# Column layout of the projection banks in a Hedgehog-attention plus MLP kernel, and one transpose for the later row statistics

## The chip, the cores and the metric

The kernel runs on one core of one Trainium2 chip. The metric is the device time of one launch in microseconds (us). The kernel before the change was run three times: 738.21, 738.29 and 739.31 us, median 738.29 us.

## What is computed

One layer over 2048 tokens of width 640 computes `x + attention(layernorm(x)) + mlp(layernorm(layernorm(x)))`; the second normalisation is the MLP's own.

```python
# attention: 32 heads of 20 features; the feature map is learned per head
qkv = x @ wqkv                                   # 640 -> 3 * 640
pq, pk = q @ w_phi[h], k @ w_phi[h]              # 20 x 20 per head
phi = concat(softmax(p), softmax(-p))            # 40 features per head, for q and k
kv, z = phi_k^T v, sum(phi_k)                    # over all tokens: no causal mask
o = (phi_q kv) / (phi_q z + 1e-6);  return o @ wo
# MLP: 640 -> 1728, tanh GELU, 1728 -> 640, with biases
```

## The kernel before

**Folding.** The 20 x 20 feature maps are folded into the projection weights, so that one matmul gives the map's input to the softmax. A softmax does not change when one feature is subtracted from all, so feature 0 is subtracted from the other 19 in the weights and is a constant zero: each head of q and of k is a projection of 19 columns (`DF`), and v one of 20. That gives 608 + 608 + 640 = 1856 projection columns.

**Precision.** Each fp32 operand is split into a high and a low fp32r part, the high by ScalarE (L54), the low by VectorE or GpSimd (L57). `mm3` (L62 to L65) is one product as three matmuls: high times high, high times low, low times high. Every product of 128 rows is thus three matmuls, and 640 rows are 15.

**Stages, in order of time.** (1) To about 36 us: load x, normalise, transpose the first 1024 tokens, first MLP chunks. (2) To about 225 us: the MLP over tokens 0 to 1023 (two blocks of 512, 14 hidden chunks in pairs). TensorE runs one `mm3` per kc step, and after each step calls `next(self.beside)` (L246, L288): one step of a generator that lays the preparation of the attention in between. One step of 512 columns is three matmuls. (3) From 225 to 447 us: the projections, 16 tiles of 128 tokens (L698 to L735). (4) From 447 us: the MLP over tokens 1024 to 2047, with attention, quotients and the output projection.

**The preparation generator** (`prep`, L478) runs in stage 2. For k and then q it takes six groups of six heads (the last of two), folds them (`prep_fold`, L443: matmuls of 114 columns into a bank of `Banks(3, 4)`, a split of each bank) and yields three times per half bank. The folded k goes to the resident weights `wkv_`, as does q's first group; the rest of q goes by way of a tile `t` (two buffers) to DRAM and comes back into `wq_` before stage 3 (L569 to L573). In between, statistics of the tokens 1024 to 2047 (`more_stats`). Then five chunks of v's weights are loaded into `raw` (two buffers) and split. Last, for b = 2 and 3, `rows` (L179): mean and reciprocal deviation of 512 tokens, which lie one per partition, are transposed on TensorE, copied out, stored to DRAM (L190) and loaded back broadcast to all partitions as `mr` (L192); and for each of five chunks of 128 features of x^T: load into `raw` (L508), subtract the mean on GpSimd (L518), multiply on VectorE (L521), high part on ScalarE (L525) and low part on VectorE (L528) into the two halves of a `t` tile, both stored to `y_dram` (L530). They come back as `y[b]` during stage 3.

In stages 1 and 2 the order of the instructions of TensorE, VectorE, ScalarE and GpSimd is that of the program text (`manual_schedule`, L302 and L352): an instruction that waits holds up all behind it on its engine. The DMAs all go through SyncE's queue (SP), whose order a scheduler sets; from stage 3 to the second pair of hidden chunks of stage 4 (L1007) it also sets the order on VectorE, ScalarE and GpSimd.

**A tile of stage 3** has four projections `proj(t, i)` (L585), each into one of three PSUM banks (0, 1, 2) that take turns, and, two tiles late, the product of the k features with v (`kv_tile`, L656): ten matmuls of 240 columns into banks 3 to 7 and one of 160 into the ring of three. With `CB` (L26) the four banks hold:

- i = 0: 24 heads of k (456 columns)
- i = 1: 8 heads of k (152) and 15 heads of v (300)
- i = 2: 17 heads of v (340) and 6 heads of q (114)
- i = 3: 26 heads of q (494), from `wq_`

ScalarE copies q and k from PSUM to `pks` (`evacuate`, L610; rows of 20 with feature 0 left at zero), ScalarE and VectorE split v (L652, L654). `k_tile` follows i = 1, `q_tile` the last bank with q. Both call `features` (L612): maximum and minimum per head on VectorE (L617, L618), differences on GpSimd (L628), exponential on ScalarE (L629), sums on VectorE (L631). The last tiles run as (13,0) (13,1) (13,2) (14,0) (14,1) (13,3) (15,0) (15,1) (14,3) (15,3) (14,2) (15,2), so that the last two `q_tile` come after their i = 2. The first pass of stage 4 is issued on ScalarE after the exponential of q of tile 15 (L776), and GpSimd's clearing of `kvs` and two weight splits after that tile's differences (L748, L796, L1001).

## Time and profile before

| | us |
|---|---|
| median of three runs | 738.29 |
| span of the profiled execution, first to last instruction | 736.8 |
| TensorE busy in the span | 723.8 |
| VectorE / ScalarE / GpSimd busy | 479.9 / 320.5 / 370.6 |
| stage 3 (225 to 447): VectorE / ScalarE / GpSimd busy, of 222.0 | 177.8 / 107.1 / 172.5 |

The profile gives no time outside the span; the median of the runs is 1.5 us above it. Times in the profile count from the first instruction. Matmuls are pipelined: a matmul's row is longer than its turn, so what one costs is read as the distance from one start to the next, and TensorE's busy time hides short waits. In a timeline row the bracket is the idle time before the instruction and what ended it. PE is TensorE, DVE VectorE, ACT ScalarE, POOL GpSimd, SP the queue of DMA issues.

### The profile page before, as it was taken

The page shows a single profiled execution, that of the slowest core. Times are in us where ns is not written, and L with a number is a line of the kernel's source. Part 1 is how long each engine was busy: PE and PEld are TensorE (multiplying, and loading weights), DVE is VectorE, ACT ScalarE, POOL GpSimd, SP SyncE. Part 2 cuts the span into 40 slices and gives each one's busy share as a digit, 9 for nine tenths or more (in the row PEclk, how much of TensorE's full clock was granted, in tenths as well). Part 3 has the DMA queues.
Part 4 walks back from the last instruction along what each step waited for, and adds up shares of the span by engine and source line. Part 5 has one row for each costly group of instructions (what it writes and reads, how often), then busy time and mean ns, then how long its engine had stood idle before and what let it go on. Part 6 is the DMA issues. An engine that isn't in the chain of part 4 may idle for free.

```text
span 736.8 us, 9681 instructions
## 1 busy us (share of the span) xinstructions
PE 723.8 (98%) x3441; PEld 610.2 (83%) x3441; DVE 479.9 (65%) x790; ACT 320.5 (44%) x526; POOL 370.6 (50%) x322
## 2 busy tenths in 40 slices
PE   9999999998999999999999999999999999999998
PEld 7788888777788998998998888888878888877886
DVE  7847645665653788788888788645575656767331
ACT  6624444332322464464345357256565556440110
POOL 2211222343321797797778889445586777304000
PEclk9999999999999999999999999999999999999999
DMA  9704477464543223633600706853433353153222
GB/s 317 221 19 141 143 177 178 141 193 142 159 161 144 75 86 144 161 101 150 143 0 1 179 1 200 196 149 107 126 116 114 113 157 90 48 215 127 83 84 73
DMA packets 64520, 95.36 MB, mean 129 GB/s; under 512 B 13312, under 2 KB 35216, under 8 KB 62848
## 3 DMA queue, kind: packets, MB, share of 16 engines
q1 hardware_dynamic: 64184, 94.74, 42.5%
q8 instruction: 27, 0.44, 0.3%
q14 instruction: 21, 0.17, 0.1%
q10 hardware_dynamic: 288, 0.01, 0.0%
HBM read 64.47 MB, written 30.26 MB: 129 GB/s over the span
## 4 chain that ended last, share of the span: by engine, by line
PE 73%; DVE 10%; DMA 5%; POOL 5%; ACT 3%; issue 3%; SPq 0%; POOLq 0%; DVEq 0%; ACTq 0%
PE bank L63 22%; PE bank L65 21%; PE bank L64 21%; PE bank L659 2%; PE bank L456 2%; POOL m L628 2%; PE bank L882 1%; DMA m<-r 1%; PE bank L881 1%; DVE acc L295 1%; DVE y L946 1%; DVE rx L925 1%; DVE m L57 1%; DMA raw<-in_wv 1%; DMA xb<-in_x 1%
## 5 line engine op out<-in xcount | busy, mean ns | idle before, releaser
L57 POOL TENSOR_TENSOR w<-r,w 128x640 fp32r<-128x640 f32 x52 | 83.2, 1618 | 107.6 <-ACT w L54 77.4
L63 PE MATMUL bank<-y,w 128*128 128x512 f32 (+1 forms) x334 | 131.1, 392 | 0.9 <-ACT m L250 0.6
L65 PE MATMUL bank<-y,w 128*128 128x512 f32 (+1 forms) x334 | 129.8, 389 | 0.3 <-POOL w L57 0.3
L64 PE MATMUL bank<-y,w 128*128 128x512 f32 (+1 forms) x334 | 129.6, 388 | 0.0
L63 PE MATMUL bank<-m,w 128*128 128x512 f32 x260 | 104.3, 401 | 4.6 <-DVE acc L295 3.8
L65 PE MATMUL bank<-m,w 128*128 128x512 f32 x260 | 101.8, 392 | 0.0
L64 PE MATMUL bank<-m,w 128*128 128x512 f32 x260 | 101.7, 391 | 0.0
L295 DVE TENSOR_TENSOR acc<-bank,acc 128x512 f32<-128x512 f32 x120 | 80.7, 682 | 16.7 <-PE bank L65 11.1
L57 DVE TENSOR_TENSOR m<-m,m 128x512 fp32r<-128x512 f32 (+1 forms) x54 | 45.0, 834 | 67.1 <-ACT m L54 67.1
L63 PE MATMUL bank<-wkh,y 128*128 128x456 f32 (+2 forms) x240 | 88.6, 369 | 0.0
L64 PE MATMUL bank<-wkl,y 128*128 128x456 f32 (+2 forms) x240 | 88.5, 369 | 0.0
L65 PE MATMUL bank<-wkh,y 128*128 128x456 f32 (+2 forms) x240 | 88.4, 368 | 0.0
L63 PEld LDWEIGHTS bank<-y,w 128*128 128x128 f32 x334 | 62.8, 188 | 14.1 <-DVE ob L1050 0.8
L65 PEld LDWEIGHTS bank<-y,w 128*128 128x128 f32 x334 | 62.7, 188 | 13.8 <-POOL w L57 0.7
L64 PEld LDWEIGHTS bank<-y,w 128*128 128x128 f32 x334 | 62.8, 188 | 12.7
L610 ACT ACTIVATE m<-bank 128x456 f32<-128x456 f32 (+3 forms) x64 | 27.0, 422 | 94.6 <-PE bank L65 78.2
L628 POOL TENSOR_TENSOR m<-m,mx 128x640 f32<-128x640 f32 (+2 forms) x48 | 44.5, 941 | 46.4 <-DVE mx L617 46.4
L63 PEld LDWEIGHTS bank<-m,w 128*128 128x128 f32 x260 | 48.9, 188 | 18.3 <-DVE acc L295 6.9
L875 POOL TENSOR_TENSOR e<-e,m 120x512 fp32r<-120x512 f32 (+1 forms) x28 | 38.1, 1362 | 43.2 <-ACT m L874 41.2
L65 PEld LDWEIGHTS bank<-m,w 128*128 128x128 f32 x260 | 48.8, 188 | 10.6
L631 DVE TENSOR_REDUCE sm<-m 128x64 f32<-128x1280 f32 x32 | 47.2, 1476 | 15.6 <-ACT m L629 15.5
L64 PEld LDWEIGHTS bank<-m,w 128*128 128x128 f32 x260 | 48.9, 188 | 9.6
(156 smaller groups left out, 1397.8 us busy)
## 6 DMA issues: line engine op xcount, KB each, us to landing
r<-in_w SPq DMA_DIRECT2D x52, 320.0 KB
e<-e SPq DMA_DIRECT2D x40, 240.0 KB
e<-acc SPq DMA_DIRECT2D x52, 160.0 KB
acc<-in_xT SPq DMA_DIRECT2D x4, 1280.0 KB
xb<-in_x SPq DMA_DIRECT2D x8, 320.0 KB
t<-in_x SPq DMA_DIRECT2D x8, 320.0 KB
raw<-in_xT SPq DMA_DIRECT2D x10, 256.0 KB
yh<-t SPq DMA_DIRECT2D x10, 256.0 KB
```

Source lines behind the costliest of these rows:

```text
L57: eng.tensor_tensor(lo, src, f(hi), op=ALU.subtract)
L63: nc.tensor.matmul(ps, lh, rh, start=first, stop=False, **kw)
L64: nc.tensor.matmul(ps, lh, rl, start=False, stop=False, **kw)
L65: nc.tensor.matmul(ps, ll, rh, start=False, stop=last, **kw)
L295: nc.vector.tensor_tensor(acc[b][:, m, :], pw, acc[b][:, m, :], op=ALU.add)
L456: nc.tensor.matmul(ps[:, i * kd:(i + 1) * kd], raw[:kk, (k + i) * P:(k + i + 1) * P], wpt[:kk, g, :kd // DF, 1:], start=True, stop=True)
L610: return nc.scalar.activation(p3[:, h:h + src.shape[1], 1:], src, AF.Copy).ins
L628: subs[n, t] = nc.gpsimd.tensor_tensor(ep[:, s], a, b, op=ALU.subtract)
L631: nc.vector.tensor_reduce(sm, e.rearrange("p s (h f) -> p (s h) f", f=DH), axis=AX, op=ALU.add)
L659: nc.tensor.matmul(kvp[g // 2][:VM, (g % 2) * 240:(g % 2) * 240 + 240].rearrange("p (s f) -> p s f", s=4), v[:, g * VS:g * VS + VM], ft[:, ...
L875: nc.gpsimd.tensor_tensor(pl, e, f(ph), op=ALU.subtract)
L881: nc.tensor.matmul(pn, kvs[:w, g, :], ph, start=True, stop=False)
```

## The change

The four banks of a tile get new contents. Of the 19 folded features of each head, 16 of k fill bank 0 (512 columns), and 16 of q bank 3 (512). The last 3 features of k (96 columns) and of q (96) stand in bank 1 with 15 heads of v (492 in all), and bank 2 has only v (340). `evacuate` copies a range of features of all 32 heads; bank 1 now has two such copies. `q_tile` follows i = 3 for every tile.

The preparation makes this layout: each folded half bank takes two splits, one of 16 and one of 3 features per head. All of q's first 16 features now go by way of DRAM, the rest stands in `wkv_`.

The rows of both later blocks are transposed once, as 16 rows, directly after the folding and ahead of v's weights, stored once and loaded back by two broadcasts, into tiles of their own (the second in one of the two buffers of `t`). The ten chunks of x^T run in one loop; the high part goes to one of the two halves of a `t` tile that is held throughout, and the low part is written over the chunk itself in `raw`, from where it is stored.

```diff
-CB = [24 * DF, QK + 15 * DH, QK + D + G5, 2 * QK + D]
+F1, F2 = 16 * H, 3 * H
+CB = [F1, F1 + 2 * F2 + 15 * DH, F1 + 2 * F2 + D]
...
-    def rows(b, xp, ptile):
-
-        sc = xp.tile([P, 2, 4], F32, name="sc", bufs=1)
-        nc.vector.tensor_copy(sc[:, 0, :], mv[:, 4 * b:4 * b + 4, 0])
-        nc.vector.tensor_copy(sc[:, 1, :], ry[:, 4 * b:4 * b + 4])
-        for _ in range(2):
+    def rows(xp, ptile):
+
+        sc = xp.tile([P, 2, 2, 4], F32, name="sc", bufs=1)
+        nc.vector.tensor_copy(sc[:, :, 0, :], mv[:, 8:16, 0].rearrange("p (b t) -> p b t", b=2))
+        nc.vector.tensor_copy(sc[:, :, 1, :], ry[:, 8:16].rearrange("p (b t) -> p b t", b=2))
+        for _ in range(4):
             yield
         ps = ptile()
-        nc.tensor.transpose(ps[:8, :P], sc.rearrange("p a t -> p (a t)"), idt)
...
+        nc.tensor.transpose(ps[:16, :P], sc.rearrange("p b a t -> p (b a t)"), idt)
...
+        nc.sync.dma_start(r_dram, sr)
+
+    def row_pair(b, mr):
+
+        nc.sync.dma_start(mr, r_dram[8 * b - 16:8 * b - 8].rearrange("r t -> (r t)").unsqueeze(0).to_broadcast([P, 8 * P]))
+        return mr.rearrange("p (a t) -> p a t", a=2)
...
-            split(dst[0][:, k:k + ni], dst[1][:, k:k + ni], ps[:, :ni * kd].rearrange("p (i f) -> p i f", i=ni))
+            src = ps[:, :ni * kd].rearrange("p (i h f) -> p i h f", i=ni, f=DF)
+            split(*[w[:, k:k + ni].rearrange("p c (h f) -> p c h f", f=16) for w in dst], src[:, :, :, 0:16])
+            split(*[w[:, k:k + ni, c3:c3 + 3 * nh].rearrange("p c (h f) -> p c h f", f=3) for w in wkv_], src[:, :, :, 16:])
             for _ in range(3):
                 yield
-        if n == "q" and g:
+        if n == "q":
             for p in range(2):
-                nc.sync.dma_start(wq_dram[p][:, :, (g - 1) * G5:(g - 1) * G5 + kd], f(t[:, p]))
+                nc.sync.dma_start(wq_dram[p][:, :, 96 * g:96 * g + 16 * nh], f(dst[p]))
...
+        finish(more)
+        yield from rows(fp, mlp.px)
+        hi_lo = fp.tile([P, 2, KC, G5], F32R, name="t").rearrange("p a c f -> p a (c f)")
+        mrs = [row_pair(2, mtile(5).rearrange("p a t -> p (a t)")),
+               row_pair(3, fp.tile([P, 2, KC, G5], F32, name="t").rearrange("p a c f -> p (a c f)")[:, :8 * P])]
...
-        for b in range(2, 4):
-            mr = yield from rows(b, fp, mlp.px)
-            ahead = load(b, 0)
-            for _ in range(7):
-                yield
...
-                hl = fp.tile([P, 2, KC, G5], F32R, name="t").rearrange("p a c f -> p a (c f)")[:, :, :512]
-                nc.scalar.activation(hl[:, 0], xc, AF.Copy)
-                for _ in range(2):
-                    yield
-                nc.vector.tensor_tensor(hl[:, 1], xc, f(hl[:, 0]), op=ALU.subtract)
-                for p in range(2):
-                    nc.sync.dma_start(y_dram[b - 2][p][:, c, :], f(hl[:, p]))
-                yield
+        todo = [(b, c) for b in range(2, 4) for c in range(KC)]
+        ahead = load(*todo[0])
+        for _ in range(3):
+            yield
+        for i, (b, c) in enumerate(todo):
+            mr = mrs[b - 2]
+            xc, ahead = ahead, load(*todo[i + 1]) if i < 9 else None
+            nc.gpsimd.tensor_tensor(xc, xc, mr[:, 0], op=ALU.subtract)
+            for _ in range(3):
+                yield
+            nc.vector.tensor_tensor(xc, xc, mr[:, 1], op=ALU.mult)
+            for _ in range(2):
+                yield
+            hi = hi_lo[:, i % 2, :512]
+            nc.scalar.activation(hi, xc, AF.Copy)
+            for _ in range(2):
+                yield
+            nc.vector.tensor_tensor(xc.bitcast(F32R), xc, f(hi), op=ALU.subtract)
+            for p, src in enumerate((f(hi), xc)):
+                nc.sync.dma_start(y_dram[b - 2][p][:, c, :], src)
+            yield
...
         if i == 0:
-            evac = evacuate(ps, 0, 0)
+            evac = evacuate(ps, 0, slice(1, 17))
         elif i == 1:
-            evac = evacuate(ps[:, :8 * DF], 0, 24)
-            v_parts(t, (ps[:, 8 * DF:], 0, 5, G3))
+            evac = evacuate(ps[:, :F2], 0, slice(17, 20))
+            evacuate(ps[:, F2:2 * F2], pq, slice(17, 20))
+            v_parts(t, (ps[:, 2 * F2:], 0, 5, G3))
             fts[t] = k_tile(t)
         elif i == 2:
-            evac = evacuate(ps[:, 17 * DH:], pq, 0)
             v_parts(t, (ps[:, :15 * DH], 5, 5, G3), (ps[:, 15 * DH:17 * DH], 10, 1, 2 * DH))
         else:
-            evac = evacuate(ps, pq, 6)
-        if i == (3 if t < 14 else 2):
+            evac = evacuate(ps, pq, slice(1, 17))
             q_tile(t)
```

46 lines of the change are left out of this document (17 added, 29 removed).

## The prediction, made before the result was known

> **What bounds the kernel now.** I read the page first (how busy is which engine), then what TensorE waits for, window by window, then start distances of its matmuls, then the chains around the places where it waits.
>
> ```profile
> span 736.8 us, 9681 instructions
> PE 723.8 (98%) x3441; PEld 610.2 (83%) x3441; DVE 479.9 (65%) x790; ACT 320.5 (44%) x526; POOL 370.6 (50%) x322
> ```
>
> TensorE is the bound: 98% of the span. So an edit gains only by making its matmuls take shorter turns or by removing a wait of TensorE; work taken from or put on another engine costs nothing as long as TensorE does not wait for it. The busy time by stage:
>
> ```profile
> 36.00:120.00 84.00, 83.44 (x420) 69.00 (x419) 45.66 (x103) 32.01 (x60) 15.46 (x10) 1.00 0.49 129
> 120.00:218.00 98.00, 93.77 (x410) 75.73 (x409) 59.26 (x86) 35.88 (x56) 35.87 (x26) 1.00 0.52 163
> 225.00:447.00 222.00, 221.66 (x1129) 199.39 (x1128) 177.79 (x256) 107.14 (x168) 172.51 (x171) 1.00 0.32 94
> ```
>
> The columns are length, then TensorE, weight loads, VectorE, ScalarE, GpSimd, then the granted clock, which is 1.00 throughout. The projections (225 to 447) have no hole worth naming. The window 120 to 218, in which the statistics' rows and the chunks of x^T are prepared, has 4.2 us of idle TensorE. Its waits there are few (total, times, longest), and the starts beside the three that matter:
>
> ```profile
> PE bank L63 <- DVE acc L295: 2.4, 3, 1.6
> PE bank L187 <- DVE sc L183: 1.5, 2, 1.2
> ```
>
> ```profile
> 129.81 0.39 PE L65 MATMUL bank<-m,w 128*128 128x512 f32 x1
> 131.45 0.27 PE L187 MATMUL bank<-idt,sc 128*8 128x128 f32 x1 [1.24 <-DVE sc L183]
> ...
> 165.96 0.39 PE L65 MATMUL bank<-y,w 128*128 128x512 f32 x1
> 166.65 0.27 PE L187 MATMUL bank<-idt,sc 128*8 128x128 f32 x1 [0.30 <-DVE sc L183]
> ...
> 176.77 0.39 PE L65 MATMUL bank<-m,w 128*128 128x512 f32 x1
> 178.79 0.50 PE L63 MATMUL bank<-m,w 128*128 128x512 f32 x1 [1.63 <-DVE acc L295]
> ```
>
> A matmul of 512 columns takes a turn of 0.23 us (worked out below), so the start distances 1.64, 0.69 and 2.02 hold 1.41, 0.46 and 1.79 us of waiting, **3.66 us** together. The first two are the two transposes of rows: TensorE, in program order, stands before L187 until VectorE has made `sc`. The third is the second block's broadcast:
>
> ```profile
> 175.02 2.57 POOL L518 TENSOR_TENSOR raw<-raw,m 128x512 f32<-128x512 f32 x2 [7.08 <-DMA m<-r]
> ```
>
> GpSimd waited 7.08 us for `mr`; VectorE's multiply L521 stood behind that, and the accumulation L295, which frees TensorE's bank, behind the multiply.
>
> **The change, part by part.**
>
> (a) *Bank widths.* The matmul count (60 a tile) and the columns (1856) stay. What may change is the overhead of each matmul. Starts of the first matmul of five successive groups of 15 (452, 454, 494, 456 columns, then the next), and two starts 15 matmuls of 512 apart:
>
> ```profile
> 255.00 0.40 PE L63 MATMUL bank<-wkh,y 128*128 128x452 f32 x1
> ...
> 258.12 0.36 PE L63 MATMUL bank<-wkh,y 128*128 128x454 f32 x1
> ...
> 261.20 0.38 PE L63 MATMUL bank<-w,y 128*128 128x494 f32 x1
> ...
> 264.57 0.37 PE L63 MATMUL bank<-wkh,y 128*128 128x456 f32 x1
> ...
> 267.68 1.29 PE L659 MATMUL bank<-w,v 128*127 128x240 f32 x10
> ```
>
> ```profile
> 195.92 0.39 PE L63 MATMUL bank<-y,w 128*128 128x512 f32 x1
> ...
> 199.32 0.39 PE L271 MATMUL bank<-y,w 128*128 128x512 f32 x1
> ```
>
> Turns: 3.12/15 = 208 ns at 452, 3.08/15 = 205 at 454, 3.37/15 = 225 at 494, 3.11/15 = 207 at 456, and 3.40/15 = 227 at 512. From 454 to 494 a column costs 0.49 ns; from 494 to 512 only 0.11. So 512 columns, a full bank and whole rows of 2 KB, are about 6 ns cheaper than the line through the odd widths (494 at 225 plus 18 columns at 0.44 = 233). The narrow side, from the chain of waits in order of time:
>
> ```profile
> 132.47 2.16 DMA r<-sr
> ...
> 146.04 3.94 DMA raw<-in_xT
> ...
> 169.94 4.92 DMA m<-r
> ...
> 253.96 1.12 PE bank L659 x10
> 267.84 1.12 PE bank L659 x10
> ...
> 416.20 3.15 DMA e<-acc
> ```
>
> Ten matmuls of 240 columns take 1.12 us, 112 ns each with their weight loads, so 340 columns meet no floor: from 112 at 240 and 205 at 454 (0.435 ns a column) they take 156 ns. 492 takes 224. A tile's 60 matmuls now take 3.12 + 3.08 + 3.37 + 3.11 = 12.68 us; after, 15 x (227 + 224 + 156 + 227) = 12.51. Bounds: with 512 at 231 to 233 ns nothing is gained; with 340 at 150 and 492 at 220 some 0.25 us. I take 0.12 a tile, times 16: **-1.9 us** (0 to -4.0).
>
> [...]
>
> Does the rest of a tile keep up? A period is 267.84 - 253.96 = 13.88 us and VectorE is busy 178 of 222 us, GpSimd 173: covered, by 20%. The copies on ScalarE move the same 1216 columns in four instructions. Of the bank ring, bank 1 loses: it must be free after i = 2 and i = 3, 3.08 + 3.37 = 6.45 us now, 15 x (156 + 227) = 5.75 then. Cost taken: nothing; if VectorE's low part of v comes over 2 us late, some tenths a tile.
>
> (b) *Rows in one go, directly after the folding.* Both waits for `sc` and the wait behind the second broadcast go: **-3.66 us**. The broadcasts (4.92 us) now start ahead of v's five chunks, some 15 steps before they are used; a step is three matmuls, 0.68 us, so 10 us. What is late next? Two things. v's loads share the DMA engines with 1 MB of broadcasts and stand on SP's queue beside a load that waits for the rows' store (2.16 us); behind a late chunk stands L57 on VectorE, and behind it L295.
>
> And the low part now lies in `raw`: the next load into that buffer waits until the store has landed, not only until L528 is done. The store of 256 KB to DRAM is not shown as a duration; the nearest rows are stores of 4 KB (2.16 us) and of 160 KB (3.15 us). I take 2.3, near the small one, since the store of 160 KB (`store_phi`) writes runs of 512 bytes and this one runs of 2 KB; bounds 2.0 and 4. The relay from one use of a buffer to its next is then: L528, store, load, L518, L521, L525, L528.
>
> ```profile
> L518 POOL TENSOR_TENSOR raw<-raw,m x10: 1280/1291/1752, 138.4 to 196.8; 128x512 f32<-128x512 f32 x10
> L521 DVE TENSOR_TENSOR raw<-raw,m x10: 677/683/2039, 139.8 to 200.1; 128x512 f32<-128x512 f32 x10
> L525 ACT ACTIVATE t<-raw x10: 616/634/635, 141.8 to 200.9; 128x512 fp32r<-128x512 f32 x10
> L528 DVE TENSOR_TENSOR t<-raw,t x10: 675/682/1233, 145.0 to 204.0; 128x512 fp32r<-128x512 f32 x10
> ```
>
> 2.3 + 3.94 + 1.29 + 0.68 + 0.63 + 0.68 = 9.5 us, and about 1 us for other instructions ahead on VectorE and for semaphores: 10.5. The program gives two turns of 8 steps, 16 x 0.68 = 10.9 us. So it just holds on average, but its store and load (6.24 us) do not fit in the 9 steps less L528 between (5.4), so GpSimd starts about 0.8 us late and, after the 0.75 us of slack ahead of L521, VectorE a little. I take **+0.8 us** for both (bounds 0 and +12). The three shorter waits in this window, 1.1 us by their brackets, I leave as they are.
>
> [...]
>
> (c) *End of the projections.* `q_tile` of tile 15 starts after i = 3, not i = 2.
>
> ```profile
> 439.63 0.58 ACT L610 ACTIVATE m<-bank 128x494 f32<-128x494 f32 x1 [0.29 <-PE bank L65]
> ...
> 446.08 0.25 ACT L610 ACTIVATE m<-bank 128x114 f32<-128x114 f32 x1
> ...
> 453.55 1.28 ACT L250 ACT_TABLE_LOAD   x1
> ```
>
> ```profile
> 455.58 0.51 PE L63 MATMUL bank<-y,w 128*128 128x512 f32 x1 [0.55 <-ACT m L250]
> ```
>
> Its last input comes at 439.6 instead of 446.1, 6.5 us earlier; the first GELU waits for its exponential and TensorE 0.55 us for the GELU. GpSimd is nearly full there, so the exponential gains less than 6.5 us, but 0.55 suffices. Against it, the last banks are 1.5 us shorter together, so that v of tile 14 must be split within one bank of 340 before `kv_tile`. I take **-0.5 us** (-0.7 to +1).
>
> (d) *Twice the splits in the folding.*
>
> ```profile
> L54 ACT ACTIVATE wkh<-bank 128x456 fp32r<-128x456 f32 x6 | 3.3, 553 | 18.5 <-PE bank L456 18.5
> L54 ACT ACTIVATE wkh<-bank 128x114 fp32r<-128x114 f32 x6 | 1.6, 260 | 5.5 <-PE bank L456 5.5
> ```
>
> ```profile
> L57 DVE TENSOR_TENSOR wkl<-bank,wkh 128x456 fp32r<-128x456 f32 x6 | 3.8, 630 | 5.8 <-ACT wkh L54 3.7 <-issue 2.1
> L57 DVE TENSOR_TENSOR wkl<-bank,wkh 128x114 fp32r<-128x114 f32 x6 | 1.6, 270 | 0.7 <-ACT wkh L54 0.7
> ```
>
> From the two widths an instruction's fixed part is 553 - 456 x 0.857 = 162 ns on ScalarE and 150 on VectorE. 24 more on each are 3.9 and 3.6 us, spread over 84 us in which they are busy 32 and 46: hidden behind TensorE's matmuls, except where VectorE is already late: **+0.2 us** (0 to +1). If the cover were gone, 3.6. Two more stores for q's first group ride on SP and cost nothing.
>
> Sum: -1.9 - 3.66 + 0.8 - 0.5 + 0.2 = -5.1 us on a span of 736.8; against the median of 738.29, taking the 1.5 us around the span as constant, **733.2 us**.
>
> **The rivals.** *Rival 1, no gain from the widths*: all of (a) is nothing, as where 512-wide turns cost 232 here (the stationary operand and the address are others than in the MLP). For it: same columns, same count. Against: 227 is the steady value of the 512-wide groups. 735.1 us. *Rival 2, the rows' gain is given back*: lateness of v's loads or of the relay makes TensorE wait as long as the 3.66 us removed; with (a) 736.0, together with rival 1 about 738. For it: GpSimd's 7.08 us above was a wait for a DMA, and the change adds waits for DMAs. *Rival 3, slower*: the relay takes x us over its 10.9. The ten chunks are four relays after the first two, and about 2 us of lateness are absorbed by the three banks of the second products, so it costs 4x - 2. It outweighs the 5.9 us of the rest from x = 2.0, a relay of 12.9 us, as with a store of 3.15 us, a load of 4.9 and 1 us of queue on GpSimd behind weight splits. At x = 3.5: 12 - 5.9 = +6.1, 744.4 us. Against it: load 3.94 and store near 2.16 where nothing else moves. *Rival 4*: the change doesn't do what it says, TensorE's waits for `sc` only move: within rival 2.
>
> **How the numbers follow.** Forecast (733.2, spread 730 to 734.5) 0.45; rival 1 0.17; rival 2 0.13 alone (736.0, to 737) and 0.11 with rival 1 (738); rival 3 0.14. 0.2%, about what a measurement of this kernel can tell from no change, is 1.5 us: faster means under 736.8, slower over 739.8. Faster: 0.45 + 0.17 + 0.09 = 0.71; same: 0.04 + 0.11 = 0.15; slower 0.14. The range 729.5 to 739.5 leaves out rival 3 and some 0.04 below.
>
> **What would show it.** (a) A tile's period 13.88 becomes about 13.76, with 512-wide starts 227 ns and 340-wide 156 ns apart. (b) No wait of over 0.3 us at the one transpose; no idle GpSimd before L518 for `m<-r`; idle before L518 for `raw<-in_xT` of about 1 us each. (c) No wait for L250 near 455. Wrong would make it: 512-wide turns of 232 (rival 1), waits `PE bank L63 <- DVE acc L295` in 120 to 190 that sum to over 4 us (rivals 2, 3), or a wait of TensorE for a bank in the projections.

## The result and the profile after

The changed kernel takes **739.32 us** (median of 20 runs, 738.65 to 742.56), the kernel before 738.19 us beside it (20 runs, 737.26 to 739.61): ratio 1.0016, 95% interval 1.0008 to 1.0023. So it is no faster, if anything 1.1 us slower, and not 5.1 us faster as forecast. The lines below have moved by one to ten: L54 of before is L55, L57 is L58, L63 to L65 are L64 to L66, L129 is L130, L293 is L295, L295 is L297, L456 is L459, L518 is L528, L639 is L647, L654 is L662, L659 is L667.

The head of the page of after:

```profile
span 737.6 us, 9732 instructions
...
PE 721.1 (98%) x3440; PEld 603.5 (82%) x3440; DVE 480.2 (65%) x811; ACT 324.3 (44%) x550; POOL 368.6 (50%) x322
```

TensorE's share looks unchanged, and that is all that the head can say: it is an average over stages that went in opposite directions. Busy time by stage of after, with the columns as before:

```profile
36.00:120.00 84.00, 80.39 (x398) 66.75 (x397) 46.84 (x120) 33.52 (x80) 15.44 (x10) 0.98 0.43 124
120.00:218.00 98.00, 95.60 (x419) 77.88 (x418) 60.93 (x86) 36.79 (x59) 34.92 (x25) 1.00 0.50 168
225.00:447.00 222.00, 220.12 (x1137) 192.54 (x1137) 178.84 (x262) 108.43 (x169) 173.63 (x176) 1.00 0.32 97
```

In 36 to 120 TensorE is idle 3.6 us where it was 0.6 (84 less the busy time, in both). In 120 to 218 it is the other way: 2.4 instead of 4.2. In 225 to 447, where there was no hole, there are 1.9 us now. Where a matmul record is missing from a trace, such a difference takes it for idle time, so the ledger goes by fixed points of the program instead: the first and the last of the 120 folding matmuls, the first matmul of a projection, and the last of the 160 of `kv_tile`. Of before (a row by line: count, shortest, median and longest in ns, first and last start in us; then a start):

```profile
L456 PE MATMUL bank<-wpt,raw x120: 261/275/298, 52.9 to 116.1; 120*128 120x114 f32 x100, 40*128 40x38 f32 x20
...
L659 PE MATMUL bank<-w,v x160: 269/275/377, 253.8 to 454.7; 128*127 128x240 f32 x160
```

```profile
225.39 0.36 PE L63 MATMUL bank<-wkh,y 128*128 128x456 f32 x1
```

The same of after:

```profile
L459 PE MATMUL bank<-wpt,raw x120: 261/275/422, 52.6 to 120.7; 120*128 120x114 f32 x100, 40*128 40x38 f32 x20
...
L667 PE MATMUL bank<-w,v x160: 269/275/377, 255.5 to 456.4; 128*127 128x240 f32 x160
```

```profile
227.31 0.39 PE L64 MATMUL bank<-wkh,y 128*128 128x512 f32 x1
```

| stage | before, us | after, us | difference |
|---|---|---|---|
| start to the first folding matmul | 52.9 | 52.6 | -0.3 |
| folding (to its last matmul) | 63.2 | 68.1 | **+4.9** |
| rows and chunks (to the first projection) | 109.3 | 106.6 | **-2.7** |
| projections (to the last `kv_tile` matmul) | 229.3 | 229.1 | -0.2 |
| the rest, to the end of the span | 282.1 | 281.2 | -0.9 |

The sum is +0.8, as the spans (736.8 and 737.6) have it. The stages' differences are several times the sum. Each is looked at in turn.

**Folding.** What the engines wait for in 53 to 82, of after:

```profile
ACT wkh L55 <- DVE wkl L58: 11.5, 8, 3.0
DVE wkl L58 <- ACT wkh L55: 4.0, 10, 1.7
...
PE bank L64 <- DVE acc L295: 1.8, 2, 1.1
PE bank L64 <- DVE acc L297: 1.8, 1, 1.8
```

The same window of before:

```profile
ACT wkh L54 <- PE bank L456: 22.6, 9, 8.4
```

Before, ScalarE waits for the bank that TensorE fills, then copies; nothing else. Now it also waits for VectorE, eight times, up to 3.0 us. One such place, of after:

```profile
76.56 0.64 DVE L297 TENSOR_TENSOR acc<-bank,acc 128x512 f32<-128x512 f32 x1
77.11 0.25 DVE L58 TENSOR_TENSOR wkl<-bank,wkh 128x96 fp32r<-128x96 f32 x1
77.25 0.50 PE L64 MATMUL bank<-m,w 128*128 128x512 f32 x1 [1.78 <-DVE acc L297]
77.39 0.18 ACT L55 ACTIVATE wkh<-bank 128x18 fp32r<-128x18 f32 x1 [3.02 <-DVE wkl L58]
77.61 0.18 DVE L58 TENSOR_TENSOR wkl<-bank,wkh 128x18 fp32r<-128x18 f32 x1 [0.25 <-ACT wkh L55]
```

The first split's subtraction (96 columns) ends at 77.36; only then does ScalarE copy the second part (18 columns), although the bank was filled 3 us earlier, and VectorE stands until that copy is done. The two engines read one PSUM bank in turns: copy, subtract, copy, subtract, as the program text has it. In this stage the order is the text's, so all that stands behind on VectorE, the accumulations that free TensorE's banks among it, waits too.

The accumulation at 76.56, for which TensorE waits here, stands ahead of this pair, so it is late by the turns before. It comes 3.0 us later than its like in before (there at 73.57). 1.2 us of that were there at 65.43, where VectorE's next statistics had waited longer for a load of x (64.20 in before). Most of the rest are waits at the turns between, as at 67.93 and 74.24, 0.30 us each, and one for a square root (`sr`) that ScalarE has behind a copy which had itself waited:

```profile
70.02 0.19 ACT L55 ACTIVATE wkh<-bank 128x18 fp32r<-128x18 f32 x1 [1.97 <-DVE wkl L58]
...
71.75 0.20 DVE L144 RECIPROCAL rr<-sr 128x8 f32<-128x8 f32 x1 [0.54 <-ACT sr L143]
```

One thing comes on top. TensorE's clock, of after, just behind that wait:

```profile
53.00:78.00 25.00, 21.39 (x110) 17.52 (x110) 16.76 (x48) 9.36 (x24) 3.10 (x2) 1.00 0.40 117
78.00:81.40 3.40, 3.40 (x13) 3.02 (x13) 2.66 (x8) 0.49 (x1) 0.00 (x0) 0.52 0.64 216
```

For 3.4 us the granted clock (third last column) is 0.52, and 13 matmuls are on record there. In q_late (below), the same folding without the dip, it is 1.00 in that stretch with 21. That accounts for the 0.98 of the stretch 36 to 120.

**Projections.** Starts of the first matmul of each bank and of two successive `kv_tile`, of after:

```profile
255.53 1.28 PE L667 MATMUL bank<-w,v 128*127 128x240 f32 x10
...
256.73 0.42 PE L64 MATMUL bank<-wkh,y 128*128 128x492 f32 x1
...
260.06 0.32 PE L64 MATMUL bank<-wkh,y 128*128 128x340 f32 x1
...
262.37 0.39 PE L64 MATMUL bank<-w,y 128*128 128x512 f32 x1
...
269.18 1.05 PE L667 MATMUL bank<-w,v 128*127 128x240 f32 x8
```

Turns: 3.33/15 = 222 ns at 492 columns, 2.31/15 = 154 at 340, and for the two banks of 512, which follow each other, 6.81/30 = 227. The period is 13.65 us against 13.88: 0.23 less, times 16 is 3.7 us. Yet the stage as a whole is only 0.2 shorter, so some 3.5 us were lost again. TensorE's two long waits, of after:

```profile
446.05 0.83 PE L667 MATMUL bank<-w,v 128*127 128x240 f32 x5 [1.37 <-DVE v L662]
...
455.24 0.93 PE L667 MATMUL bank<-w,v 128*127 128x240 f32 x6 [1.40 <-DVE w L58]
```

Both stand at the last two `kv_tile`. Behind the second is GpSimd's order, of after:

```profile
443.82 1.43 POOL L636 TENSOR_TENSOR m<-m,mx 128x600 f32<-128x600 f32 x2
...
446.57 1.58 POOL L58 TENSOR_TENSOR w<-r,w 128x640 fp32r<-128x640 f32 x1
448.08 1.29 POOL L804 MEMSET kvs<- 120x1408 f32 x1
449.32 2.37 POOL L647 TENSOR_TENSOR m<-m,w 128x1280 f32<-128x1280 f32 x1
```

and of before:

```profile
442.98 2.37 POOL L639 TENSOR_TENSOR m<-m,w 128x1280 f32<-128x1280 f32 x1 [0.48 <-DVE w L637]
```

The weighting of k's features of tile 15, which the last `kv_tile` needs, came before the last differences of q's features. Now q's inputs are there earlier, and the weighting stands behind differences, a weight split and the clearing of `kvs`, 6.3 us later.

**Rows and chunks.** The long load, of after:

```profile
129.20 2.40 SPq L505 DMA_DIRECT2D raw<-in_wv  x2
...
135.06 0.74 ACT L55 ACTIVATE wkh<-raw 128x640 fp32r<-128x640 f32 x1 [3.41 <-DMA raw<-in_wv]
135.83 0.82 DVE L58 TENSOR_TENSOR wkl<-raw,wkh 128x640 fp32r<-128x640 f32 x1 [3.45 <-ACT wkh L55]
...
139.18 0.50 PE L64 MATMUL bank<-m,w 128*128 128x512 f32 x1 [1.50 <-DVE acc L297]
```

The waits for `sc` and behind the second broadcast are gone, and the three shorter ones too; two new ones (start distances 1.7 and 1.1 us over the turn, at 137 and 140) come from a load of v's weights, the first of the two issues in the first row, that was issued behind 1 MB of broadcasts; the split could start at 135.06, almost 5.9 us later.

### The profile page after: what moved, and what is told of

Same layout as the page of the kernel before. It is cut to its first block, busy times and chain, and to the rows that moved or that the text cites. A ratio compares the mean times of both kernels' runs of the same rounds, so it can differ in the third digit from the quotient of the medians.

```text
span 737.6 us, 9732 instructions
## 1 busy us (share of the span) xinstructions
PE 721.1 (98%) x3440; PEld 603.5 (82%) x3440; DVE 480.2 (65%) x811; ACT 324.3 (44%) x550; POOL 368.6 (50%) x322
## 4 chain that ended last, share of the span: by engine, by line
PE 87%; DVE 7%; DMA 3%; ACT 2%; issue 1%; SPq 0%; DVEq 0%; ACTq 0%
PE bank L64 26%; PE bank L66 25%; PE bank L65 25%; PE bank L667 2%; PE bank L459 2%; PE bank L889 1%; PE bank L888 1%; DVE st L130 1%; DMA raw<-in_wv 1%; DVE y L953 1%; DMA t<-in_x 1%; PE bank L274 1%; PE bank L273 1%; PE bank L824 1%; DVE y L58 0%
## 5 line engine op out<-in xcount | busy, mean ns | idle before, releaser
L58 POOL TENSOR_TENSOR w<-r,w 128x640 fp32r<-128x640 f32 x52 | 83.5, 1622 | 109.1 <-ACT w L55 75.6
L64 PE MATMUL bank<-y,w 128*128 128x512 f32 (+1 forms) x334 | 130.9, 392 | 0.4 <-DVE ob L1057 0.4
L66 PE MATMUL bank<-y,w 128*128 128x512 f32 (+1 forms) x334 | 129.8, 389 | 0.0
L65 PE MATMUL bank<-y,w 128*128 128x512 f32 (+1 forms) x334 | 129.7, 388 | 0.0
L64 PE MATMUL bank<-m,w 128*128 128x512 f32 x260 | 104.7, 403 | 7.6 <-DVE acc L297 5.1
L66 PE MATMUL bank<-m,w 128*128 128x512 f32 x260 | 102.3, 394 | 0.0
L65 PE MATMUL bank<-m,w 128*128 128x512 f32 x260 | 102.0, 392 | 0.0
L297 DVE TENSOR_TENSOR acc<-bank,acc 128x512 f32<-128x512 f32 x120 | 80.3, 682 | 16.1 <-PE bank L66 10.4
L64 PE MATMUL bank<-wkh,y 128*128 128x512 f32 (+2 forms) x240 | 87.5, 365 | 0.0
L66 PE MATMUL bank<-wkh,y 128*128 128x512 f32 (+2 forms) x240 | 87.0, 363 | 0.0
L65 PE MATMUL bank<-wkl,y 128*128 128x512 f32 (+2 forms) x240 | 87.0, 363 | 0.0
L58 DVE TENSOR_TENSOR m<-m,m 128x512 fp32r<-128x512 f32 (+1 forms) x54 | 44.0, 815 | 56.4 <-ACT m L55 56.4
L64 PEld LDWEIGHTS bank<-y,w 128*128 128x128 f32 x334 | 62.8, 188 | 13.5 <-DVE ob L1057 0.8
L66 PEld LDWEIGHTS bank<-y,w 128*128 128x128 f32 x334 | 62.7, 188 | 12.9
L65 PEld LDWEIGHTS bank<-y,w 128*128 128x128 f32 x334 | 62.9, 188 | 12.7
L64 PEld LDWEIGHTS bank<-m,w 128*128 128x128 f32 x260 | 49.2, 189 | 21.6 <-DVE acc L297 7.8
L618 ACT ACTIVATE m<-bank 128x512 f32<-128x512 f32 (+1 forms) x64 | 26.4, 439 | 86.3 <-PE bank L66 60.6
L252 ACT ACTIVATE m<-bank,b1t 128x512 f32<-128x512 f32 (+1 forms) x54 | 36.2, 670 | 50.6 <-PE bank L66 44.9
L639 DVE TENSOR_REDUCE sm<-m 128x64 f32<-128x1280 f32 x32 | 47.3, 1478 | 17.0 <-ACT m L637 16.8
L66 PEld LDWEIGHTS bank<-m,w 128*128 128x128 f32 x260 | 49.0, 188 | 10.5
```

What stands on the lines that cost most here:

```text
L58: eng.tensor_tensor(lo, src, f(hi), op=ALU.subtract)
L64: nc.tensor.matmul(ps, lh, rh, start=first, stop=False, **kw)
L65: nc.tensor.matmul(ps, lh, rl, start=False, stop=False, **kw)
L66: nc.tensor.matmul(ps, ll, rh, start=False, stop=last, **kw)
L252: nc.scalar.activation(gt, pz, AF.Gelu_apprx_tanh, bias=b1t[:, 2 * g + j:2 * g + j + 1])
L297: nc.vector.tensor_tensor(acc[b][:, m, :], pw, acc[b][:, m, :], op=ALU.add)
```

## The experiments

Each kernel's time is the median; the ratio is to the kernel before on the same chip. The stages are measured at the fixed points above.

| kernel | us | ratio, 95% interval | folding | rows | projections | rest |
|---|---|---|---|---|---|---|
| before | 738.19 | | 63.2 | 109.3 | 229.3 | 282.1 |
| after | 739.32 | 1.0016 [1.0008, 1.0023] | 68.1 | 106.6 | 229.1 | 281.2 |
| two_splits_on_before | 743.48 | 1.0061 [1.0049, 1.0074] | 67.5 | 109.6 | 229.3 | 282.1 |
| fold_pairs | 736.70 | 0.9981 [0.9972, 0.9990] | 64.7 | 107.0 | 229.3 | 281.2 |
| pairs_on_before | 739.84 | 1.0017 [1.0009, 1.0026] | 64.8 | 109.0 | 229.3 | 282.1 |
| q_late | 739.31 | 1.0012 [1.0003, 1.0020] | 67.4 | 107.1 | 229.0 | 281.2 |
| k15_first | 737.99 | 0.9992 [0.9983, 1.0001] | 67.3 | 107.2 | 227.3 | 281.2 |
| v14_first | 736.74 | 0.9974 [0.9963, 0.9985] | 67.9 | 106.4 | 225.7 | 282.0 |
| rows_old | 740.82 | 1.0031 [1.0019, 1.0044] | 67.2 | 108.8 | 229.1 | 281.2 |
| rows_new_on_before | 736.78 | 0.9983 [0.9973, 0.9993] | 63.3 | 107.2 | 229.3 | 282.1 |
| bcast_late | 739.13 | 1.0012 [1.0003, 1.0021] | 67.2 | 106.8 | 229.0 | 281.3 |
| bcast_gated | 739.24 | 1.0005 [0.9996, 1.0013] | 68.0 | 106.3 | 229.1 | 281.2 |
| gated_low_own | 738.72 | 1.0005 [0.9997, 1.0014] | 68.1 | 105.5 | 229.1 | 281.4 |
| pairs_v14 | 733.26 | 0.9938 [0.9925, 0.9950] | 64.7 | 106.7 | 225.9 | 281.2 |
| pairs_v14_x_first | 732.42 | 0.9933 [0.9919, 0.9947] | 63.5 | 107.5 | 226.0 | 281.2 |
| pairs_v14_gated_low_own | 732.21 | 0.9920 [0.9907, 0.9933] | 64.7 | 105.5 | 225.7 | 281.3 |

Where a part is not edited, its stage says how far a stage repeats: the changed folding gives 67.2 to 67.4 where the clock stays at 1.00 (q_late, k15_first, rows_old, bcast_late) and 67.9 to 68.1 where it dips behind the wait at 75 us (after, v14_first, bcast_gated, gated_low_own), the new rows 106.4 to 107.5, the old ones 108.8 to 109.6, the last two columns agree to 0.3, except for the rest of v14_first: 282.0, where pairs_v14, with the same edit of q's features, has 281.2. TensorE waits 0.4 us for `km` there, which it doesn't in pairs_v14; the cause is open.

**two_splits_on_before.** Does the folding alone cost it? The kernel before, with two splits a bank and nothing else:

```
-            split(dst[0][:, k:k + ni], dst[1][:, k:k + ni], ps[:, :ni * kd].rearrange("p (i f) -> p i f", i=ni))
+            src = ps[:, :ni * kd].rearrange("p (i h f) -> p i h f", i=ni, f=DF)
+            for fs_ in (slice(0, 16), slice(16, DF)):
+                split(*[w[:, k:k + ni].rearrange("p c (h f) -> p c h f", f=DF)[:, :, :, fs_] for w in dst], src[:, :, :, fs_])
```

> The kernel before with one edit: each folded half bank is split in two parts, 16 and 3 features per head, high part, low part, high part, low part, into the old columns. No other part of the change. Theory A: this edit alone makes VectorE late in the folding and accounts for the 3.6 us of additional waits that the changed kernel shows between 53 and 120 us; the time goes from 738.3 to about 742 us. Rival B: the waits come of the new stores and of the widths, or are taken up later by waits that the kernel before has anyway in 120 to 218 us; 738.3 to 739.5 us.

Measured: 4.9 us slower, the folding 4.3 us longer, with the mutual waits of after:

```profile
ACT wkh L54 <- DVE wkl L57: 11.3, 8, 3.0
DVE wkl L57 <- ACT wkh L54: 4.1, 10, 1.7
```

So the second split alone makes the whole loss in the folding; widths, rows and the layout of k have no part in it.

**fold_pairs.** Is it the number of instructions, or the turns of the two engines at the bank? The changed kernel with the same instructions in another order, both copies ahead of both subtractions:

```
-            split(*[... for w in dst], src[:, :, :, 0:16])
-            split(*[... for w in wkv_], src[:, :, :, 16:])
+            parts = [([... for w in dst], src[:, :, :, 0:16]),
+                     ([... for w in wkv_], src[:, :, :, 16:])]
+            for (hi, lo), s in parts:
+                nc.scalar.activation(hi, s, AF.Copy)
+            for (hi, lo), s in parts:
+                nc.vector.tensor_tensor(lo, s, f(hi), op=ALU.subtract)
```

> The changed kernel, but in the folding both high parts of a half bank are made first (two ScalarE instructions), then both low parts (two VectorE instructions); the same 24 additional instructions on each engine. Theory A (hand-offs): in the changed kernel the second ScalarE copy waits until VectorE has made the first low part, and VectorE waits again for that copy; these waits in the folding made VectorE late and TensorE waited 4.5 us for it between 53 and 120 us. Then TensorE's waits there fall to under 1.5 us and the time from 739.3 to about 736.3 us. Rival B (amount of work): the 24 additional instructions themselves, 3.6 us of VectorE, are the cost; the waits stay at 4 us or more and the time at 739.3 +- 0.5 us.

Measured: 736.70 us, 2.6 less than after; the folding 64.7 instead of 67.2 to 68.1, with the clock at 1.00 throughout. In 53 to 82 ScalarE waits for TensorE's bank alone again:

```profile
ACT wkh L465 <- PE bank L459: 22.1, 8, 8.4
...
DVE st L130 <- DMA t<-in_x: 2.8, 2, 1.5
```

The turns of the two engines are most of the loss: the accumulation that came at 76.56 in after comes at 74.78, the 1.2 us late that belong to the load of x. The records of after show them: in 53 to 82 each second part's copy that follows a subtraction from its bank starts about 0.03 us after that one's end, as at 77.39 (77.36), and the two never overlap on one bank. Why a copy waits for a subtraction that only reads another part of the bank is not shown. Some 1.5 us over the 63.2 of before remained.

**pairs_on_before and pairs_v14_x_first.** What are the 1.5 us: the number, or the load of x, for which VectorE now waits (the last row above)? First the kernel before with the folding of fold_pairs and nothing else:

> The kernel before with each bank of the folding split in two parts, both copies ahead of both subtractions; banks, rows and the rest as before. Theory, the number of instructions costs what is left (2.4 us of waits against 0.9): about 1.5 us over the kernel before, 740.0 us, ratio 1.002, waits of 0.7 to 0.9 us near 66, 68 and 74 us. Rival, the number costs nothing and the order of SP's queue does it: as before, 738.4 us, waits in 53 to 120 us under 1.2 us together.

Measured: 739.84 us, folding 64.8. The theory's number came, but it doesn't tell the two apart as meant: SP's queue has the order of after in this kernel too (a load of wk at 56.0 and a second at once behind it, which holds the queue to 61.7; x after that). In the kernel before, a load of x came ahead of the second:

```profile
61.28 0.33 SPq L473 DMA_DIRECT2D t<-in_x  x1
61.70 0.39 SPq L440 DMA_DIRECT2D raw<-in_wkT  x1
```

The scheduler sets that order, and the second split alone shifts it. The other kernel puts it back. It has fold_pairs and v14_first (below), and this:

```
-            ahead = raws(*jobs[i + 1]) if i < 11 else None
+            if i != 2:
+                ahead = raws(*jobs[i + 1]) if i < 11 else None
...
+                if i == 2 and k == 1:
+                    with tc.issue_after(xl[2].ins):
+                        ahead = raws(*jobs[3])
```

`xl[2]` is the third of the loads of x; what is issued within `issue_after` is placed behind the named instruction on its engine, without a wait.

> The changed kernel with copies ahead of subtractions and q's features of tiles 14 and 15 held (733.3 us as measured), and on SP's queue the load of x for the third later tile of the statistics ahead of the fourth load of wk, as the kernel before has it. Theory, the order of the queue: the wait of 0.80 us at 66.2 us goes, and what follows it shrinks, 732.0 to 732.6 us. Rival, the number of instructions: all three waits stay, 733.3 us.

Measured: folding 63.5, 1.2 us less than in pairs_v14, and 732.42 us against 733.26. SP's queue in pairs_v14_x_first, and its row of the folding:

```profile
61.10 0.33 SPq L484 DMA_DIRECT2D t<-in_x  x1
61.52 0.39 SPq L442 DMA_DIRECT2D raw<-in_wkT  x1
```

```profile
L459 PE MATMUL bank<-wpt,raw x120: 260/275/299, 52.6 to 116.1; 120*128 120x114 f32 x100, 40*128 40x38 f32 x20
```

In pairs_v14 the order is the other one:

```profile
55.98 5.63 SPq L442 DMA_DIRECT2D raw<-in_wkT  x2
61.70 4.86 SPq L482 DMA_DIRECT2D t<-in_x  x3
```

So of the folding's 4.0 to 4.9 us the alternation at the bank takes 2.5 to 2.7, the dip of the clock behind its longest wait 0.7 where it occurs, the order of the loads 1.2, and the number of instructions with all the rest about 0.3: near what (d) had for it. The saving in the span is only 0.4 us (731.1 to 730.7), since the rows stage is 0.8 longer in that run; the intervals of the two ratios overlap.

**q_late, k15_first, v14_first.** What makes the two waits at the last `kv_tile`? The first moves `q_tile` in the program text, so that tile 15's follows i = 2 again:

```
+        if i == (3 if t < 14 else 2):
             q_tile(t)
```

> The changed kernel, but the query features of tiles 14 and 15 are put after their bank i = 2 again, as in the kernel before. Theory A: starting them two banks earlier puts their GpSimd and VectorE work ahead of the weighting of tile 15's key features and of the split of tile 14's values, for which TensorE then waits 1.5 and 1.6 us at the two last products of key features with values. Then both waits go, the wait of 0.55 to 0.7 us for the first GELU comes back, and the time falls by 2.3 us to 737.0. Rival B: the last two banks, 340 columns each instead of 454, leave too little time for the split of tile 14's values; the first of the two waits stays at 0.8 us or more and the time is 737.8 to 738.6 us.

Measured: nothing (739.31 us, projections 229.0), and GpSimd's weighting of tile 15 still starts at 449. In this stage the scheduler sets the order of VectorE, ScalarE and GpSimd, and it sets the same one. The run tells nothing of the theory; it tells that a move in the text is no experiment there. So the order itself was fixed, for tile 15 first:

```
+            with ExitStack() as gate:
+                for name in ("recip", "mult") if t == 15 else ():
+                    gate.enter_context(tc.issue_after(marks[name, 15].ins))
                 q_tile(t)
```

`marks` holds the reciprocal and the weighting of k's features of tile 15.

> The changed kernel, with the query features of tile 15 queued on VectorE behind the reciprocal and on GpSimd behind the weighting of tile 15's key features (issue order only). The place of the query features in the program text alone changed nothing, since the scheduler sets the order there. Theory A: of the two waits of TensorE near 444 and 453 us, the second (1.6 us) comes from this weighting, which the change put behind the differences of tiles 14 and 15 and the clearing of kvs; it goes, the first stays at 1.5 us, some of the GELU's wait (0.7) may come back: 737.7 to 738.5 us. Rival B: the second wait comes from something else on the way (the high part on ScalarE behind the GELU); it stays at 1 us or more, 739.3 us.

Measured: 737.99 us, projections 227.3, 1.8 us less; the wait at the last `kv_tile` is gone, the one at that of tile 14 stays:

```profile
PE bank L667 <- DVE v L662: 1.4, 1, 1.4
PE bank L667 <- DVE w L58: 0.5, 1, 0.5
```

(the 0.5 is a wait at about 415 us that before has too, with 0.3). v14_first has this and, as q_late, the moved `q_tile`, with q of tile 14 behind the high part and q of tile 15 behind the low part of tile 14's v:

```
+            gates = {14: [("hi", 14)], 15: [("recip", 15), ("mult", 15), ("lo", 14)]}
```

> As k15_first, and in addition the exponential of tile 14's query features is queued on ScalarE behind the high parts of tile 14's values, and tile 15's query features on VectorE behind the low parts. Theory A: both waits of TensorE (1.5 and 1.6 us) go and the GELU's 0.7 comes back at most: 736.3 to 737.0 us. Rival B: two banks of 340 columns leave too little time for the split of the values whatever the order; the first wait stays at 0.8 us or more: 737.8 to 738.6 us.

Measured: 736.74 us, projections **225.7**, with only the 0.5 left. So both waits come from q's features that got ahead, and v of tile 14 is not late because its bank is short: the banks are as narrow as in after. 229.3 - 225.7 = 3.6 us is now the widths' whole gain, as the period has it. GpSimd's weighting of tile 15 starts at 443.4 there, ahead of the last differences, and not at 449.3.

**rows_old, rows_new_on_before.** What is the rows' part worth? Once undone in the changed kernel, once alone in the kernel before (the diff is the rows' part of the change, shown above, taken back or alone).

> The changed kernel with the preparation of the later rows and of the chunks of x^T as in the kernel before (a transpose for each block of 512 tokens, low part in a tile of its own); the column layout is the new one. Theory A: the rows' part by itself is worth what its waits show: it removed 3.7 us at the transposes and the second broadcast and about 1.5 us of other waits, and it added 2.7 us behind late loads of the value weights. Then undoing it costs 2.4 us: 741.7 us. Rival B: TensorE's waits in 120 to 218 us depend on how late VectorE comes out of the folding, not on how the rows are made; the time stays at 739.3 +- 0.7 us.

> The kernel before with the rows part alone: both later blocks' rows transposed in one go after the folding, low part over the chunk's own buffer; bank widths, folding and end of the projections as before. Theory: it is worth what its undoing cost in the changed kernel, 1.5 us, with the late loads of v taking back some 2.7 us: 736.5 to 737.5 us. What the prediction had: 2.9 us, 735.7 us. Rival: without the wider banks of v beside it no load comes late in time to hold TensorE, and the whole 3.66 us is won: 734.9 us.

Measured: 740.82 us, 1.5 more than after, between what its two theories had; and 736.78 us, 1.6 less than before, the rows stage 107.2 instead of 109.3. In rows_old the waits for `sc` are back; of rows_new_on_before TensorE's waits in 120 to 218 are, in all:

```profile
PE bank L63 <- DVE acc L296: 2.6, 2, 1.7
```

The two agree: about 2 us of the stage, 1.5 to 1.6 of the time. The waits for `sc` go, and the late load of v comes with the rows' part alone; the wide banks are not needed for it.

**bcast_late, bcast_gated, gated_low_own.** Can the late load be avoided? bcast_late moves the two broadcasts in the text to v's last chunk:

> The changed kernel, but the two broadcasts of the rows are issued in the program only after the last load of the value weights. Theory A: the value weights are late because their loads stand on the DMA queue behind a broadcast that waits for the rows' store, and share the DMA engines with 1 MB of broadcasts; the split of the third chunk then comes 3.5 us late on VectorE and TensorE waits 1.7 and 1.1 us. Then these two waits go and the time falls to about 736.6 us. Rival B: the loads are late by their own two buffers (load, copy, split, next load take longer than the three steps given to a chunk), as before the change; the waits stay at 1.5 us or more and the time is 738.3 to 739.5 us.

Measured: nothing; SP's queue has them at the same place, since the scheduler sets it. As q_late, no test. bcast_gated fixes the order with `issue_after` behind v's last load:

```
+            if kc == KC - 1:
+                gate = tc.issue_after(loads[-1].ins)
+                gate.__enter__()
+                mrs = [...]
+                gate.__exit__(None, None, None)
```

> The changed kernel with the two broadcasts of the rows queued on SP behind the last load of the value weights; moving them in the program text alone left them where they were in the queue. Theory A: the third load of value weights took 5.8 us from issue to landing beside the broadcasts instead of 2.8 to 3.4, so its split stood 3.5 us on VectorE and TensorE waited 1.7 and 1.1 us; with the broadcasts later the load takes about 3 us, these waits fall under 0.8 us in all and the time is about 737.3 us. Rival B: the loads are late by their two buffers; waits stay at 2 us or more, 739.3 us. Rival C: the broadcasts now come late for GpSimd, and TensorE waits 1 us or more some 10 us later instead; 738.5 us.

Measured: 739.24 us. The load now keeps the split waiting 0.5 us and not 3.4:

```profile
131.95 0.74 ACT L55 ACTIVATE wkh<-raw 128x640 fp32r<-128x640 f32 x1 [0.52 <-DMA raw<-in_wv]
...
152.41 0.50 PE L64 MATMUL bank<-m,w 128*128 128x512 f32 x1 [1.03 <-DVE acc L297]
...
180.91 0.50 PE L64 MATMUL bank<-m,w 128*128 128x512 f32 x1 [0.94 <-DVE acc L297]
```

The waits at 137 and 140 are gone, and two others, 1.2 and 1.1 us by start distances, are there in the chunk loop. The gain is given back. gated_low_own asks whether those come from the relay: the low part goes to a tile of its own, so that a load no longer waits for a store, and the second block's broadcast comes after the fifth chunk.

```
-            nc.vector.tensor_tensor(xc.bitcast(F32R), xc, f(hi), op=ALU.subtract)
-            for p, src in enumerate((f(hi), xc)):
+            nc.vector.tensor_tensor(lo, xc, f(hi), op=ALU.subtract)
+            for p, src in enumerate((f(hi), f(lo))):
```

> The changed kernel with the broadcasts held until v's last chunk is loaded (that run: waits of 1.19 us at 151 and 1.10 us at 180, 739.2 us in all), and the low part of a chunk written to a tile of its own as before, so that a load waits for the subtraction and not for the store; the second block's rows are broadcast after the fifth chunk. Theory, the relay (L528's load waits for the store) makes the two waits: they go, a wait of up to 1 us at the change of blocks may stay, GpSimd's idle time ahead of L528's operation for the load falls from 19 us to under 8: 737.0 to 738.0 us. Rival, the two waits come from the late broadcast and not from the relay: they stay, 739.2 us. Second rival: the second broadcast, after the fifth chunk, brings back the 1.8 us that the change took away: 740 us or more.

Measured: 738.72 us, rows stage 105.5, outside what the theory had. The wait at 151 is gone; one of 1.4 us stands at 179. Some 10 us ahead of it GpSimd waited for the second broadcast:

```profile
169.44 1.28 POOL L532 TENSOR_TENSOR raw<-raw,m 128x512 f32<-128x512 f32 x1 [7.69 <-DMA m<-r]
```

That this makes the wait at 179 is not shown: two weight splits (3.55 us) stand between them on GpSimd. The stage is 0.8 us shorter than in bcast_gated, no more than the new rows vary by, and the two times don't tell the two kernels apart. How much of the waits in the chunk loop the relay makes stays open.

**pairs_v14, pairs_v14_gated_low_own.** Do the repairs add?

> The changed kernel with both edits that took a wait of TensorE away: in the folding both copies of a bank ahead of both subtractions, and at the end of the projections q's features of tiles 14 and 15 held until tile 14's v is split and tile 15's weights are multiplied. Theory: the losses in the folding (2.6 us measured alone) and at the end (2.6 us alone) are two mechanisms in two stages and add: 739.3 - 5.2 = 734.1 us, ratio 0.994. Rival: both only shift one chain that ends at the same place, so the second edit brings less once the first is made: 736 to 737 us.

> All four edits on the changed kernel: copies ahead of subtractions, q's features of tiles 14 and 15 held, broadcasts held until v's chunks are loaded, low part in a tile of its own. If all are separate: 739.3 - 2.6 - 2.6 - 1.8 = 732.3 us, ratio 0.9915. Rival, the two edits of the rows bring nothing: 734.1 us. Rival, they cost: 735 us or more.

Measured: 733.26 us with the folding and the end of the projections repaired, 6.1 less than after (2.6 and 2.6 by themselves), and 732.21 us with the rows' edits too. The first two add (the dip of the clock may be what is over), so these were separate mechanisms in separate stages. The 1.1 us of the rows' edits are not told from nothing: the two intervals overlap. With the repairs the change is worth 5 to 6 us against before: ratio 0.9920 [0.9907, 0.9933] for the best.

## Why the prediction was wrong

**The step that failed is (d)**, "twice the splits in the folding": "hidden behind TensorE's matmuls, except where VectorE is already late: +0.2 us (0 to +1). If the cover were gone, 3.6." It cost 4.0 to 4.9 us. The fixed parts (24 more instructions by 162 and 150 ns) were sized rightly: about 0.3 us shows when all else is taken out. What was left out is an order. A split is a copy by ScalarE and a subtraction by VectorE from one PSUM bank, and these take turns (in 53 to 82 of after the waiting engine starts 0.03 to 0.04 us behind the other's end); two splits in a row make four turns in place of two, and each engine's turn comes after whatever stands ahead of it in program order. The second copy started only when VectorE was through with the first subtraction, after waiting up to 3.02 us (at 77.39), and that subtraction stands behind statistics and accumulations. In (b) the prediction asked what is queued behind each wait that the change adds; in (d) it took instructions to be loads on an engine and never asked whether they wait for each other. The second loss there, 1.2 us, is a step of which it had nothing: a different split makes the scheduler put a load of wk ahead of one of x.

**(c)** "-0.5 us (-0.7 to +1)" was wrong in sign: the wait for the first GELU went (the rest of the span is 0.9 us shorter), but at the last two `kv_tile` 3.4 us were lost. It named the place for v of tile 14 and priced it too low, and put the cause in the narrow bank, which v14_first refutes. One of its signs of being wrong, a wait of TensorE for a bank in the projections, is what came. It had "GpSimd is nearly full there" and drew from it only that the exponential gains less. In after GpSimd is busy all 16.0 us from 436 to 452, in an order that a scheduler sets, and what came earlier pushed k's weighting back by 6.3 us.

**(a)** "-1.9 us (0 to -4.0)" had the mechanism right and the size too small by half. 512-wide turns came at the forecast 227 ns, 340 and 492 at 154 and 222 for 156 and 224. These alone make 12.45 us a tile in place of 12.68. The forecast's own numbers gave 12.51, that is 0.17 a tile; it took 0.12, a hedge toward the bound of nothing. The other bound was added up too small: 15 x (227 + 220 + 150 + 227) is 12.36, that is 0.32 a tile and not 0.25. Rival 1, no gain from the widths, is refuted: the same columns in the same number of matmuls take 3.6 us less.

**(b)** "-3.66 and +0.8" is -2.9; the stage lost 2.7 in after and 2.1 to 2.2 over the runs, and 1.5 to 1.6 of the time. The waits that were to go went. The sum is nearly right for two reasons that cancel: the late load of v, the first of the two things named as late next, costs 2.7 us, where 0.8 was taken for it and the relay together; and the three shorter waits, left as they were, went as well. The relay, for which the bound was +12, made no wait of TensorE in after: GpSimd waits for the loads, as said, and longer than said,

```profile
POOL raw L528 <- DMA raw<-in_xT: 19.4, 5, 5.0
```

but TensorE waits for nothing behind it in 150 to 218. The 2.3 us for the store fit: the loads of x^T that wait for a store of 256 KB are issued 2.0 to 2.8 us after it. That the length of the runs makes the difference to the 3.15 us of the other store was the author's estimate and is not shown. Rival 3 did not occur. Rival 2 has the right shape, the gain of one part given back by late data, but not the size: the rows kept most of theirs.

So the total of 739.3 is no single rival. It is -3.6 from the widths and -2.7 from the rows against +4.9 from the folding and +2.5 from the end of the projections (3.4 lost, 0.9 won), the two parts that were costed at a few tenths.

## What to carry to other kernels

An instruction added on an idle engine is free only if it waits for nobody (24 more on each of two engines cost about 0.3 us here, and their turns at the bank 2.5 to 2.7): before costing it by its duration, write down the order in which the engines reach a shared bank or tile, and put all of one engine's reads ahead of the other's. Work that is made ready earlier can be moved in front of something else where a scheduler sets the order and an engine is full (k's weighting came 6.3 us later), and what is moved back has to be looked up with its due time; there, too, an experiment has to fix the order itself, for moving the text changed nothing twice. When a change moves the total little, set fixed points in the program and difference the stages: here +4.9, -2.7, -0.2 and -0.9 stood behind +0.8.

## What the runs showed that was not expected

- The longest wait in the folding may have cost more than its length. Behind it (1.95 us at 75, start distance over the turn) the clock fell in four of the nine profiles that have that wait, to 0.52 for 3.4 us in after and to 0.50 to 0.58 in 78 to 80 and 0.57 to 0.70 in 80 to 82 over the four, and these foldings are 0.5 to 0.9 us longer; where the wait is 0.6 to 0.7 us, as in before and fold_pairs, it fell in none. What decides it is open: in 74 to 78 TensorE was busy 2.2 of 4 us in after, and as long in two_splits_on_before, where the clock stayed at 1.00. That the wait brings the fall about is not shown: of the executions of which no trace was kept, one of fold_pairs (739.08 us against the median of 736.70) and two of rows_new_on_before (739.01 and 739.23 against 736.78) have a mean clock of 0.995, though the profiles of these kernels have no such wait at 75; where it fell there is unknown.
- A hand-over at a shared PSUM bank is visible by itself: VectorE stands 0.25 us for ScalarE's copy of 18 columns (0.18 us), as the row at 77.61 shows, and 0.30 us for one of 72 (0.23 us), so that in both some 0.07 us come on top of the copy.
- Matmul turns: 340 to 492 columns, (222 - 154)/152 = 0.45 ns a column; 492 to 512, (227 - 222)/20 = 0.25. The last 20 columns of a bank are cheaper again, as the 494 and 512 of before had it (0.11).
- A load of 320 KB took up to 5.9 us when it was issued 0.9 us behind two broadcasts of 512 KB each, and in bcast_gated, without them ahead of it, its data were there about 3.0 us after the issue (128.94 to 131.95).
